# One order out of 401 planned ones, and a shorter way to split V, in a three-layer attention kernel

## The chip, the cores and the metric

One NeuronCore of one Trainium2 chip. The metric is the device time of one launch in microseconds (us). The kernel before took 1083.33 us (median of 3 runs, 1083.30 to 1086.17).

## The reference

Three layers follow each other, for 4 batches (b = 0..3) of 448 positions and a width of 768:

```python
scores = scale * np.matmul(q, k.transpose(0, 1, 3, 2))      # causal, 12 heads of 64
attn = softmax(mask(scores));  x = concat(attn @ v)          # 1. attention
h = xt @ U @ V;  u = x + h.T                                 # 2. low-rank mixing over positions
x = u + np.maximum(u @ w_ch1, 0.0) @ w_ch2                   #    and an MLP of 768 -> 3072 -> 768
logits = x @ w_gate;  top 2 of 4 experts                     # 3. each expert: one causal attention head
out += gate[e] * (softmax(mask(q @ k.T)) @ v) @ wo[e]
```

All is float32. The kernel multiplies in pieces of float16: a float32 operand is split into a high part (rounded to float16) and a low part (what is left), and three products of such parts (high*high, high*low, low*high) replace one.

## The kernel before

**Steps.** `ORDER` lists the work: `a0` to `a3` are the attention of a batch (`attention(b)`, six pairs of heads each, so pairs 0 to 23 in all), `mgb..` is weight group g (of 4) of the MLP for batches b (`mlp`), `s2` and `s3` are groups 2 and 3 for batches 2 and 3 together by a seven-product scheme (`strassen`), `e0` to `e3` are the experts. The list starts a0 a1 m00 m01 m101.

**A pair of heads** (`attention`, L693): the scores come from TensorE; VectorE adds the mask and takes the maximum (the profile's CUSTOM_DVE_ANT_0); ScalarE takes the exponential and copies the high part in float16; GpSimd subtracts for the low part (`softmax`, L512); two transposing DMAs from SP's queue turn the result. `prep(n)` (L490) splits V of the pair: ScalarE scales V in place (112x512), ScalarE copies the high part (112x8x64), GpSimd subtracts for the low part (112x8x64). `weighted` (L589) first calls `shares` (the reciprocals of the sums: small 112x8 operations on VectorE, 16 small matmuls of shape 64x112 on TensorE, one copy on ScalarE), then makes 24 products of V and the turned scores (64x448 to 64x112); VectorE multiplies the two, ScalarE and GpSimd split the result, and a transposing DMA and `lowrank(n)` (L606; 12 matmuls of 64x128, two ScalarE copies, 32x128 on VectorE, one more matmul) end the pair.

**Weights.** Each of the 48 weight tiles (`weight_tile`, L743) is loaded, decoded on VectorE (four passes of 128x768), squared on ScalarE, normed by a matmul of 128x1, scaled and rounded on ScalarE, and cut on GpSimd (two of 128x384). Tiles 0 to 11 (group 0) are due during the attention of batches 0 and 1.

**What sets the order.** No operation is issued when the code calls it. `Program.add` records it with its engine, its dependencies and a key (the due time, `prog.key`; `HT` = 4500 per half pair; matmuls of the MLP get `FILL`, a key so late that they go wherever nothing else is ready). `Program.issue` (L203) then runs a list schedule: it keeps a clock for each engine, made of `cost` (L125) and `LATENCY` (L59), always takes the engine that can start first, lets it issue its ready operation of the smallest key, and so lays down one fixed sequence per engine. On the chip every engine works through its sequence in order and waits on semaphores. Where the planned TensorE would idle for over 100 ns before 210 us (`WARM_END`, L43) the planner puts dummy matmuls of 128x448 into TensorE's sequence (L1248, called fillers below); they keep its clock up. The plan itself orders nothing across engines.

Of the kernel before, what the change touches and what calls it, by code (L numbers as in the profile page):

```python
# [3 lines left out]

# [42 lines left out]
NE = 6  # L47
ORDER = "a0 a1 m00 m01 m101 m20 m30 e0 a2 m21 m31 e1 a3 m02 m12 s2 s3 e2 m03 m13 e3"
NT = 2 * NG * GF + NE
PASS = [(0, 0), (0, 1), (1, 0)]  # L50


class Program:
# [2 lines left out]

    LATENCY = {"pe": 197.0, "act": 135.0, "dve": 185.0, "pool": 85.0, "sp": 1010.0}  # L59

    def __init__(self):
        self.ops = []
# [59 lines left out]
            self.state[r] = ([], [])  # L122
        return self.near[r]

    def cost(self, name, method, outs, ins, kw):  # L125
        o = outs[0]
        n = 1
        for c in o.shape[1:]:
            n *= c
        if name == "pe":  # L130
            f = 4.0 if ins[0].dtype == F32 else 1.0
            c = f * max(n / 2.4 + 2.5, 36.0)
            self.work = c * (ins[0].shape[0] / 128.0) * (o.shape[0] / 128.0)

            return c * (0.62 if HD in (o.shape[0], ins[0].shape[0]) and n >= C else 1.0)
        ptr = sum(x.free_size() == 1 and n > 1 for x in ins)
        psum = any(a.space == bass.MemoryType.PSUM for a in outs + ins)
        if name == "act" and method == "dma_start":
            return 300.0
        if name == "act":  # L140
            src = 51.0 if ins[0].space == bass.MemoryType.PSUM else 94.0
            return src + n / 1.2 + 93.0 * (ptr + len(outs) - 1)
        if name == "dve":
            m = 1
            for c in ins[0].shape[1:] if ins else o.shape[1:]:
                m *= c
# [3 lines left out]
            return (64.0 + (m / 2 if fast else m)) / 0.96 + 64.0 * ptr + 80.0 * (self.port and n > 32)  # L150
        if name == "pool":
            if method == "partition_all_reduce":
                return 374.0
            self.port = True
            return 150.0 + 2.0 * n if method == "tensor_tensor" else 260.0 + 2.5 * n
        return 350.0 + outs[0].nbytes() / 292.0 if method == "dma_start_transpose" else 650.0

    def add(self, name, method, fn, a, k):
        outs, ins = [], []
        for key, x in list(enumerate(a)) + list(k.items()):  # L160
            if hasattr(x, "ap"):
                (outs if key in (0, "out", "accum_out") else ins).append(x)
        self.work, self.port = 0.0, False
        cost = self.cost(name, method, outs, ins, k)
        data = 0.0
        if method.startswith("dma"):
            nbytes = max(x.nbytes() for x in outs + ins)
            data = nbytes / (292.0 if method == "dma_start_transpose" else 360.0)
        deps = set()
        i = len(self.ops)  # L170
        if self.group_op:
            i -= 1
        for x in ins:
            r = self.region(x)
            if r is not None:
                for q in self.touching(r):
                    deps.update(self.state[q][0])
                self.state[r][1].append(i)
        for x in outs:
            r = self.region(x)  # L180
            if r is not None:
                for q in self.touching(r):
                    w, rd = self.state[q]
                    deps.update(w)
                    deps.update(rd)
                    if q[1] >= r[1] and q[2] <= r[2] and q[3] >= r[3] and q[4] <= r[4]:
                        w[:] = [i]
                        rd[:] = []
        deps.discard(i)
        if self.group_op:  # L190
            op = self.ops[-1]
            op["calls"].append((fn, a, k))
            op["cost"] += cost
            op["work"] += self.work
            op["deps"] |= deps
        else:
            op = dict(eng=name, cost=cost, data=data, deps=deps, calls=[(fn, a, k)], key=self.key,
                      work=self.work, port=self.port)
            self.ops.append(op)
            if self.group_op is False:  # L200
                self.group_op = True

    def issue(self):  # L203
        ops = self.ops
        left = [len(o["deps"]) for o in ops]
        users = [[] for _ in ops]
        for i, o in enumerate(ops):
            for d in o["deps"]:
                users[d].append(i)
        at = [0.0] * len(ops)  # L210
        names = ["pe", "act", "dve", "pool", "sp"]
        free = dict.fromkeys(names, 0.0)
        bus = port = 0.0
        warm, window, load = False, 0.0, 0.0
        waiting = {n: [] for n in names}
        ready = {n: [] for n in names}
        for i, o in enumerate(ops):
            if not left[i]:
                heapq.heappush(waiting[o["eng"]], (0.0, i))
        done = 0  # L220
        while done < len(ops):
            best = None
            for n in names:
                t = free[n]
                while waiting[n] and waiting[n][0][0] <= t:
                    i = heapq.heappop(waiting[n])[1]
                    heapq.heappush(ready[n], (ops[i]["key"], i))
                if not ready[n]:
                    if not waiting[n]:
                        continue  # L230
                    t = waiting[n][0][0]
                if best is None or t < best[0]:
                    best = (t, n)
            t, n = best
            while waiting[n] and waiting[n][0][0] <= t:
                i = heapq.heappop(waiting[n])[1]
                heapq.heappush(ready[n], (ops[i]["key"], i))
            i = heapq.heappop(ready[n])[1]
            o = ops[i]
            if n == "pe" and self.idle and t < WARM_END:  # L240
                u = free[n] or WARM_START
                while u + WARM_GAP < t:
                    while u > window + WINDOW:
                        warm = load > (0.42 if warm else 0.76) * WINDOW
                        window, load = window + WINDOW, 0.0
                    self.idle()
                    c = 190.0 if warm else 380.0
                    u += c
                    load += c
                t = max(t, u)  # L250
            for fn, a, k in o["calls"]:
                fn(*a, **k)  # L252
            done += 1
            cost = o["cost"]
            if n == "pe":
                while t > window + WINDOW:
                    warm = load > (0.42 if warm else 0.76) * WINDOW
                    window, load = window + WINDOW, 0.0
                load += o["work"] * (1.0 if warm else 2.0)
                if not warm:  # L260
                    cost *= 2.0

            if o["port"]:
                t = max(t, port)
                port = t + cost
            end = t + cost
            free[n] = end
            if o["data"]:
                end = bus = max(bus, t + 1290.0) + o["data"]
                if n == "sp" and cost > 700.0:  # L270
                    free[n] = max(free[n], end - 1000.0)
            for u in users[i]:
                gap = 20.0 if n == "pe" and ops[u]["eng"] == "pe" else self.LATENCY["sp" if o["data"] else n]
                at[u] = max(at[u], end + gap)
                left[u] -= 1
                if not left[u]:
                    heapq.heappush(waiting[ops[u]["eng"]], (at[u], u))
        return max(free.values())


@with_exitstack
def kernel(
# [207 lines left out]
    def prep(n):  # L490
# [804 lines left out]
```

## Time and profile before

| | |
|---|---|
| Median of the runs | 1083.33 us |
| The profiled execution: time, span | 1087.6 us, 1085.6 us |
| Busy: TensorE / VectorE / ScalarE / GpSimd | 1043.5 / 695.1 / 639.6 / 484.7 us |
| of TensorE's busy time: fillers (L1248) | 436 matmuls, 96.2 us |
| Mean granted clock of TensorE | 0.995 |

The span runs from the first to the last instruction; the execution's time is 2 us longer. A busy TensorE is not a useful one here, since fillers count as busy. So the profile is read by stretches: up to 219.5 us (attention of batches 0 and 1 with group 0 for batch 0 between it), where fillers stand, and after it, where TensorE's own work follows without a break but for short waits.

### The profile page before, as it was taken

Reading aid. Unit: us, or ns where it says so; the run is one execution under the profiler, and the core shown is the slowest. Engines: PE = TensorE matmul, PEld = TensorE weight load, DVE = VectorE, ACT = ScalarE, POOL = GpSimd, SP = SyncE. Lnnn points to the kernel's source line nnn. Section 1 sums busy time; section 2 is a strip of 40 time slices with the busy share of each in tenths; the row PEclk is TensorE's granted clock in tenths of the full one; section 3 lists DMA queues with packets and bytes.
Section 4 is the critical chain, followed back from the end, with each engine's and each line's share of the span. In section 5 each row is a group of like instructions: output and inputs, shape, how many; then the busy total and the mean of one; then the engine's idle time right before and its main releaser. Section 6 shows DMA issues by size and latency. Waiting matters only on the chain.

```text
span 1085.6 us, 18934 instructions
## 1 busy us (share of the span) xinstructions
PE 1043.5 (96%) x6824; PEld 556.0 (51%) x6824; DVE 695.1 (64%) x1811; ACT 639.6 (59%) x1517; POOL 484.7 (45%) x528
## 2 busy tenths in 40 slices
PE   8999999999999999999999999999999999999996
PEld 3455454555545555554455554455455544555554
DVE  6778698878767677535566545577665768432363
ACT  3898998566754654447885448884462631631163
POOL 1777766325424331024563016674697992220011
PEclk9999999999999999999999999999999999999998
DMA  5999899746868876547997257995434444543024
GB/s 165 231 246 231 214 216 235 208 167 225 283 229 285 279 271 235 172 116 177 244 243 156 88 116 179 224 193 128 129 112 139 131 123 154 145 116 102 18 77 94
DMA packets 220141, 192.56 MB, mean 177 GB/s; under 512 B 176304, under 2 KB 179504, under 8 KB 220048
## 3 DMA queue, kind: packets, MB, share of 16 engines
q1 hardware_dynamic: 220048, 191.36, 64.7%
q8 instruction: 53, 0.87, 0.3%
q14 instruction: 40, 0.33, 0.1%
HBM read 112.16 MB, written 36.18 MB: 137 GB/s over the span
## 4 chain that ended last, share of the span: by engine, by line
PE 66%; DMA 14%; ACT 8%; POOL 5%; DVE 4%; issue 2%; SPq 0%; DVEq 0%; ACTq 0%; POOLq 0%
PE bank L252 62%; DMA arena<-arena 9%; ACT arena L252 8%; POOL arena L252 5%; PE bank L1248 4%; DVE arena L252 4%; DMA arena<-w 2%; DMA w<-arena 2%; DMA arena<-in_w_dram 1%; DMA arena<-in_wv_dram 1%; DMA arena<-in_v_dram 1%; DMA out_dram<-arena 0%; SPq L252 0%; DMA arena<-in_qk_dram 0%; ACT bank L252 0%
## 5 line engine op out<-in xcount | busy, mean ns | idle before, releaser
L252 PE MATMUL bank<-arena 128*128 128x448 f16 (+10 forms) x6388 | 957.7, 326 | 36.4 <-DMA arena<-arena 12.3
L252 POOL TENSOR_TENSOR arena<-arena 112x112 f16<-112x112 f32 (+8 forms) x517 | 482.5, 956 | 590.7 <-ACT arena L252 544.5
L252 PEld LDWEIGHTS <-arena 128*128 128x128 f16 (+4 forms) x5852 | 474.8, 104 | 430.0 <-issue 82.9
L252 ACT ACTIVATE arena<-arena 128x448 f16<-128x448 f32 (+11 forms) x895 | 492.8, 587 | 272.0 <-DVE arena L252 192.2
L252 DVE CUSTOM_DVE_ANT_0 arena<-bank,arena 112x112 f32<-112x112 f32 (+4 forms) x280 | 124.4, 476 | 71.9 <-PE bank L252 57.2
L252 DVE TENSOR_TENSOR arena<-bank,arena 128x448 f16<-128x448 f32 (+2 forms) x160 | 94.8, 600 | 117.3 <-ACT arena L252 90.9
L252 DVE SCALAR_TENSOR_TENSOR arena<-arena 128x768 int32<-128x768 int32 (+6 forms) x168 | 163.1, 988 | 2.0 <-ACT arena L252 0.9
L252 DVE SCALAR_TENSOR_TENSOR arena<-bank,arena 128x448 f32<-128x448 f32 (+1 forms) x138 | 84.2, 621 | 88.0 <-PE bank L252 69.2
L252 DVE TENSOR_SCALAR arena<-arena 128x1 int32<-128x1 int32 (+8 forms) x377 | 88.5, 258 | 41.2 <-ACT arena L252 15.6
L252 ACT ACTIVATE arena<-bank 128x448 f16<-128x448 f32 (+2 forms) x148 | 75.1, 520 | 59.7 <-PE bank L252 58.7
L252 DVE TENSOR_TENSOR arena<-arena 112x8 f16<-112x8 f32 (+10 forms) x136 | 88.5, 664 | 18.3 <-ACT arena L252 16.7
L1248 PE MATMUL bank<-arena 128*128 128x448 f16 x436 | 96.2, 362 | 1.9 <-DVE arena L1172 1.0
L252 ACT ACTIVATE arena<-bank,arena 64x128 f16<-64x128 f32 (+2 forms) x97 | 41.6, 433 | 56.3 <-PE bank L252 51.1
L252 ACT ACTIVATE bank<-bank,arena 128x448 f32<-128x448 f32 x72 | 43.0, 602 | 53.5 <-PE bank L252 52.2
L252 PEld LDWEIGHTS bank<-arena 64*112 64x112 f32 (+5 forms) x536 | 48.2, 173 | 48.3 <-issue 15.4
L1248 PEld LDWEIGHTS <-arena 128*128 128x128 f16 x436 | 40.9, 102 | 47.1 <-issue 14.8
L252 DVE TENSOR_REDUCE arena<-arena 128x1 f32<-128x448 f32 (+8 forms) x107 | 57.5, 545 | 6.8 <-DMA arena<-in_v_dram 2.9
L252 ACT ACTIVATION_READ_ACCUMULATOR arena<-arena 112x1 f32 (+1 forms) x304 | 57.4, 189 | 0.0
L252 DVE DVE_READ_ACCUMULATOR2_ANT arena<- 112x1 f32 (+1 forms) x280 | 22.9, 82 | 0.0
L252 DVE CAST arena<-arena 112x8 f16<-112x8 f32 x32 | 15.3, 483 | 2.2 <-PE bank L252 1.9
L252 DVE TENSOR_SCALAR arena<-bank 128x1 f32<-128x1 f32 x48 | 7.3, 152 | 12.7 <-PE bank L252 10.7
L252 DVE TENSOR_REDUCE arena<-bank 1x1 f32<-1x128 f32 (+2 forms) x14 | 3.9, 277 | 9.3 <-PE bank L252 9.2
(12 smaller groups left out, 17.7 us busy)
## 6 DMA issues: line engine op xcount, KB each, us to landing
arena<-w SPq DMA_DIRECT2D x138, 384.0 KB, 3.5
arena<-in_w_dram SPq DMA_DIRECT2D x48, 768.0 KB, 5.3
w<-arena SPq DMA_DIRECT2D x78, 384.0 KB, 4.3
arena<-in_qk_dram SPq DMA_DIRECT2D x24, 448.0 KB, 4.0
arena<-in_v_dram SPq DMA_DIRECT2D x24, 224.0 KB, 4.3
out_dram<-arena SPq DMA_DIRECT2D x24, 224.0 KB, 2.0
arena<-in_we_dram SPq DMA_DIRECT2D x6, 384.0 KB, 4.5
arena<-arena SPq DMA_TRANSPOSE x88, 4.7
```

Source lines behind the costliest of these rows:

```text
L252: fn(*a, **k)
L1248: prog.idle = lambda: nc.tensor.matmul(bank[:, 7, 64:512], ZERO.to_broadcast([128, 128]), ZERO.to_broadcast([128, S]), start=True, stop=True)
```

## The change

It has two parts.

1. `prep`: the in-place scaling of V on ScalarE and the subtraction on GpSimd go. `split` (L470 of before) does both steps from the loaded tile: ScalarE writes the high part with the scale, VectorE computes scale*V - high in one SCALAR_TENSOR_TENSOR of 112x8x64. Per pair: one ScalarE operation and one GpSimd operation less, one VectorE operation more; 24 pairs.
2. `Program`: `cost` and the latencies get other numbers, transposing DMAs get a model of their own, and each duration is taken times 1.03. The schedule moves into `plan(keys, users)`, which issues nothing and returns the planned end and the order. `issue` plans once, then 400 times more with the keys of 1 to 16 random groups of operations moved by random amounts (only keys of 0 to 270000, those of the attention, the weight tiles and the first steps of `strassen`), keeps the order with the earliest planned end, and issues that one. The random numbers have a fixed seed.

```diff
+STEP, MOVABLE, SEED, ROUNDS = 4500.0, 270000.0, 8, 400
...
-    LATENCY = {"pe": 197.0, "act": 135.0, "dve": 185.0, "pool": 85.0, "sp": 1010.0}
+    HOP = 66.0
+    SLACK = 1.03
...
-    def issue(self):
+    def plan(self, keys, users):
+
         ops = self.ops
...
+            cost, fill = o["cost"] * self.SLACK, 0
+            tail = o["tail"]
             if n == "pe":
+                if t < WARM_END:
+                    u = free[n]
+                    while u + WARM_GAP < t:
...
+                        fill += 1
+                        c = 190.0 if warm else 380.0
+                        u += c
+                        load += c
+                    t = max(t, u)
...
+    def issue(self):
+
+        ops = self.ops
...
+        best, order = self.plan(keys, users)
+        dice = random.Random(SEED)
+        for _ in range(ROUNDS):
+            trial = keys[:]
+            for _ in range(dice.choice((1, 2, 4, 16))):
+                by = dice.gauss(0.0, dice.choice((0.1, 0.5, 2.0))) * STEP
+                for i in dice.choice(parts):
+                    trial[i] = max(0.0, trial[i] + by)
+            end, made = self.plan(trial, users)
+            if end <= best:
+                best, order, keys = end, made, trial
+        for i, fill in order:
+            for _ in range(fill):
+                self.idle()
+            for fn, a, k in ops[i]["calls"]:
+                fn(*a, **k)
...
-        act.activation(vs, vs, AF.Copy, scale=SV[0:C, b:b + 1])
-        act.activation(dst[:, :, 0:64], src, AF.Copy)
-        pool.tensor_tensor(out=dst[:, :, 64:128], in0=src, in1=dst[:, :, 0:64], op=ALU.subtract)
+        split(dst[:, :, 0:64], dst[:, :, 64:128], src, SV[0:C, b:b + 1])
```

The program built from it has 401 fillers in place of 436, and the same 6120 other matmuls. Up to the 975th of these (the last one before group 0's work on batch 1) the sets are the same in both; their sequence is not. At three places:

ScalarE, the first two pairs, from the last small exponential on (112x224, 112x448: exponentials; 112x2x..x56: high parts; 112x512 and 112x8x64: V; 128x768: weight tile). Before:

```order
L252 ACTIVATE arena<-arena 112x224 x2
L252 ACTIVATE arena<-arena 112x2x2x56 x2
L252 ACTIVATE arena<-arena 112x512
L252 ACTIVATE arena<-arena 112x2x3x56
L252 ACTIVATE arena<-arena 112x8x64
L252 ACTIVATE arena<-arena 112x512
L252 ACTIVATE arena<-arena 112x2x3x56
L252 ACTIVATE arena<-arena 112x448 x2
L252 ACTIVATE arena<-arena 112x2x4x56
L252 ACTIVATE arena<-arena 128x768
L252 ACTIVATE arena<-arena 112x2x4x56
L252 ACTIVATE arena<-arena 112x8x64
```

and now:

```order
L324 ACTIVATE arena<-arena 112x8x64 x2
L324 ACTIVATE arena<-arena 112x224 x2
L324 ACTIVATE arena<-arena 112x2x2x56 x2
L324 ACTIVATE arena<-arena 128x768
L324 ACTIVATE arena<-arena 112x448
L324 ACTIVATE arena<-arena 112x2x3x56
L324 ACTIVATE arena<-arena 112x448
L324 ACTIVATE arena<-arena 112x2x3x56
L324 ACTIVATE arena<-arena 112x2x4x56
```

The scaling of V is gone, and V's high parts moved ahead of the larger exponentials.

VectorE, end of batch 1's attention, around pair 10's `lowrank` (32x128: its operand; the TENSOR_TENSOR just ahead of the ISA: the product of pair 11; the one ahead of that: a low part of the MLP; ISA 128x448: the sum of pair 10). Before:

```order
L252 SCALAR_TENSOR_TENSOR arena<-bank,arena 32x128
L252 COPY arena<-bank 128x1
L252 TENSOR_SCALAR arena<-bank 128x1
L252 SCALAR_TENSOR_TENSOR arena<-arena 128x768
L252 TENSOR_TENSOR arena<-bank,arena 128x448
L252 TENSOR_SCALAR arena<-arena 128x1 x2
L252 TENSOR_TENSOR arena<-bank,arena 128x448
L252 ISA arena<-bank,arena 128x448
```

and now:

```order
L324 SCALAR_TENSOR_TENSOR arena<-arena 128x768
L324 TENSOR_TENSOR arena<-bank,arena 128x448
L324 SCALAR_TENSOR_TENSOR arena<-arena 112x8x64
L324 SCALAR_TENSOR_TENSOR arena<-bank,arena 32x128
L324 TENSOR_TENSOR arena<-bank,arena 128x448
L324 ISA arena<-bank,arena 128x448
L324 ISA arena 128x1
L324 SCALAR_TENSOR_TENSOR arena<-arena 112x8x64
```

Two of the new subtractions (V of pairs of batch 2) stand here, one of them ahead of pair 10's 32x128.

TensorE, the same place (64x448 to 64x112 in one run: pair 11's products; 64x128: pair 10's `lowrank`; the later run of 64x112: pair 11's `shares`; 128x1: norm of a weight tile; 128x448: MLP). Before:

```order
L252 MATMUL bank<-arena 64x448
...
L252 MATMUL bank<-arena 64x128
L252 MATMUL bank<-arena 128x1
L252 LDWEIGHTS arena
L252 MATMUL bank<-arena 128x448
...
L252 MATMUL bank<-arena 128x1
...
L252 MATMUL bank<-arena 64x112
```

and now (L1292 are fillers):

```order
L324 MATMUL bank<-arena 64x112
L1292 LDWEIGHTS arena
L1292 MATMUL bank<-arena 128x448
...
L324 MATMUL bank<-arena 128x448
...
L324 MATMUL bank<-arena 64x128
...
L324 MATMUL bank<-arena 64x448
```

Pair 11's `shares` stood behind its products, behind pair 10's `lowrank` and behind two norms; it now stands ahead of all of them.

## Rows read from the trace of the kernel before

**Rows 1.** The page: span, then busy time, share and instructions of each engine.
```profile
span 1085.6 us, 18934 instructions
PE 1043.5 (96%) x6824; PEld 556.0 (51%) x6824; DVE 695.1 (64%) x1811; ACT 639.6 (59%) x1517; POOL 484.7 (45%) x528
```
**Rows 2.** The page's costliest groups: count, busy us, mean ns, idle before, releaser.
```profile
L1248 PE MATMUL bank<-arena 128*128 128x448 f16 x436 | 96.2, 362 | 1.9 <-DVE arena L1172 1.0
```
**Rows 3.** Busy time by stretch: length, each engine's busy us (instructions), clock, DMA share, GB/s.
```profile
20.00:182.30 162.30, 156.30 (x1215) 82.00 (x1214) 131.77 (x422) 145.52 (x405) 114.05 (x134) 1.00 0.94 218
0.00:219.50 219.50, 208.81 (x1535) 109.21 (x1536) 174.01 (x538) 173.61 (x453) 133.90 (x161) 1.00 0.90 219
219.50:1085.60 866.10, 834.68 (x5291) 446.82 (x5288) 521.08 (x1274) 466.00 (x1065) 350.81 (x367) 0.99 0.59 167
300.00:330.00 30.00, 28.27 (x146) 14.53 (x145) 21.18 (x53) 17.04 (x25) 11.31 (x11) 0.94 0.69 233
```
**Rows 4.** The chain of waits, 20 to 220 us: shares of the stretch.
```profile
by line: PE bank L252 34.0%; PE bank L1248 15.8%; DMA arena<-arena 14.1%; ACT arena L252 13.9%; POOL arena L252 10.5%; DVE arena L252 5.0%; issue 3.3%; DMA arena<-in_v_dram 2.8%; SPq L252 0.6%; ACTq L252 0.0%; POOLq L252 0.0%
```
**Rows 5.** ScalarE's and GpSimd's groups by shape, 20 to 210 us: V's three operations.
```profile
L252 ACT ACTIVATE arena<-arena 112x512 f32<-112x512 f32 x18 | 12.5, 709 | 0.3 <-DVE arena L252 0.3
L252 ACT ACTIVATE arena<-arena 112x512 f16<-112x512 f32 x14 | 8.5, 616 | 2.0 <-PE bank L252 2.0
L252 POOL TENSOR_TENSOR arena<-arena 112x512 f16<-112x512 f32 x14 | 17.2, 1233 | 1.1 <-ACT arena L252 1.1
```
**Rows 6.** VectorE's groups by shape, 20 to 210 us.
```profile
L252 DVE SCALAR_TENSOR_TENSOR arena<-arena 128x448 f16<-128x448 f32 x6 | 5.4, 904 | 0.6 <-ACT arena L252 0.5
L252 DVE CAST arena<-arena 112x8 f16<-112x8 f32 x12 | 8.8, 732 | 0.0
```
**Rows 7.** VectorE in order of time: start, length, instruction; the nearest kin of the new subtraction.
```profile
115.88 1.55 DVE L252 SCALAR_TENSOR_TENSOR arena<-arena 128x448 f16<-128x448 f32 x1
218.04 3.65 DVE L252 SCALAR_TENSOR_TENSOR arena<-arena 128x448 f16<-128x448 f32 x6
719.62 2.71 DVE L252 SCALAR_TENSOR_TENSOR arena<-arena 128x448 f16<-128x448 f32 x1
```
**Rows 8.** GpSimd in order of time, beside the first and third of rows 7.
```profile
114.81 3.24 POOL L252 TENSOR_TENSOR arena<-arena 128x448 f16<-128x448 f32 x4 [0.97 <-ACT arena L252]
718.97 4.25 POOL L252 TENSOR_TENSOR arena<-arena 112x336 f16<-112x336 f32 x4 [0.83 <-ACT arena L252]
```
**Rows 9.** TensorE by shape, 192.9 to 194.6 us: pair 11's products.
```profile
L252 PE MATMUL bank<-arena 112*64 112x448 f16 x6 | 1.2, 356 | 0.0
L252 PE MATMUL bank<-arena 112*64 112x112 f16 x6 | 0.7, 213 | 0.0
```
**Rows 10.** TensorE by shape, 196.85 to 197.6 us: pair 11's `shares`.
```profile
L252 PE MATMUL bank<-arena 112*64 112x112 f16 x16 | 0.6, 216 | 0.0
```
**Rows 11.** VectorE in order of time: the product of pair 11.
```profile
198.33 0.61 DVE L252 TENSOR_TENSOR arena<-bank,arena 128x448 f32<-128x448 f32 x1
```
**Rows 12.** TensorE in order of time, around the end of the first stretch.
```profile
215.31 1.12 PE L1248 MATMUL bank<-arena 128*128 128x448 f16 x5
216.36 0.38 PE L252 MATMUL bank<-arena 1*128 1x1 f32 x2
216.67 2.86 PE L1248 MATMUL bank<-arena 128*128 128x448 f16 x14
219.37 2.81 PE L252 MATMUL bank<-arena 128*128 128x448 f16 x14
```
**Rows 13.** TensorE's waits after 219.5 us: us in total, times, longest.
```profile
PE bank L252 <- ACT arena L252: 9.4, 11, 1.7
PE bank L252 <- DVE arena L252: 8.6, 6, 2.0
PE bank L252 <- DMA arena<-arena: 8.3, 9, 2.2
PE bank L252 <- DMA arena<-w: 1.2, 2, 0.8
```

More of the change, by code (lines that the diff above doesn't have):

```diff
@@ L216, in issue @@
         ready = {n: [] for n in names}
+        order = []
         for i, o in enumerate(ops):
@@ L219, in issue @@
                 heapq.heappush(waiting[o["eng"]], (0.0, i))
-        done = 0
-        while done < len(ops):
+        while len(order) < len(ops):
             best = None
@@ L224, in issue @@
                 t = free[n]
[L225 to L229, printed above, removed]
+                w, r = waiting[n], ready[n]
+                while w and w[0][0] <= t:
+                    i = heapq.heappop(w)[1]
+                    heapq.heappush(r, (keys[i], i))
+                if not r:
+                    if not w:
                         continue
-                    t = waiting[n][0][0]
+                    t = w[0][0]
                 if best is None or t < best[0]:
@@ L234, in issue @@
             t, n = best
[L235 to L238, printed above, removed]
-            o = ops[i]
[L240 to L254, printed above, removed]
-            if n == "pe":
+            w, r = waiting[n], ready[n]
+            while w and w[0][0] <= t:
+                i = heapq.heappop(w)[1]
+                heapq.heappush(r, (keys[i], i))
+            i = heapq.heappop(r)[1]
+            o = ops[i]
+            cost, fill = o["cost"] * self.SLACK, 0
+            tail = o["tail"]
+            if n == "pe":
+                if t < WARM_END:
+                    u = free[n]
+                    while u + WARM_GAP < t:
+                        while u > window + WINDOW:
+                            warm = load > (0.42 if warm else 0.76) * WINDOW
+                            window, load = window + WINDOW, 0.0
+                        fill += 1
[3 more added lines that the diff above has]
+                    t = max(t, u)
                 while t > window + WINDOW:
@@ L265, in issue @@
                 port = t + cost
[L266 to L271, printed above, removed]
+            free[n] = t + cost
+            end = t + cost + tail
+            if o["turns"]:
+                behind = turn > t
+                free[n] = max(t + 120.0, plain + 60.0, turn - 700.0 if behind else 0.0)
+                end = max(free[n] + 250.0, turn) + o["data"]
+                if behind:
+                    free[n] = max(free[n], end - 1800.0)
+                turn = end
+                bus = max(bus, end + 400.0)
+            elif o["data"]:
+                bus = max(bus, t + 1050.0) + o["data"]
+                end = bus + 850.0
+                plain = max(plain, end)
@@ L278, in issue @@
-        return max(free.values())
+                    heapq.heappush(waiting[e], (at[u], u))
+        return last, order
+    def issue(self):
+        ops = self.ops
+        users = [[] for _ in ops]
+        parts = {}
+        for i, o in enumerate(ops):
+            for d in o["deps"]:
+                users[d].append(i)
+            if 0.0 <= o["key"] < MOVABLE:
+                parts.setdefault((o["eng"], o["key"]), []).append(i)
+        parts = list(parts.values())
+        keys = [o["key"] for o in ops]
+        best, order = self.plan(keys, users)
[14 more added lines that the diff above has]
+                fn(*a, **k)
```

68 lines of the change are left out of this document (37 added, 31 removed).

## The prediction

> **What bounds the kernel now.** I read the page first, for the span and the busy times [rows 1]. TensorE is 96% busy, but 96.2 us of that are fillers [rows 2]. So I next took the busy times by stretch [rows 3], cut where the fillers end. Up to 219.5 us TensorE is busy for 208.8 us; without the fillers its own work is 112.6 us, and 10.7 us are idle in spite of them. That stretch costs 219.5 us for 112.6 us of work: it is bound by something else. After it, 834.7 of 866.1 us are work. The 31.4 us that are left are small waits [rows 13], the longest of 2.2 us. Whatever the change wins must therefore come from the 107 us in the first stretch that are not work, or from these 31 us.
>
> What sets the length of the first stretch? The chain of waits there [rows 4] holds, beside TensorE and its fillers, transposing DMAs (14%), ScalarE (14%), GpSimd (10.5%) and VectorE (5%): it runs through the pairs of heads, each handing its tiles around all engines, with two or three pairs under way. From 20 to 182.3 us, where the last pair's high parts are copied, ScalarE is busy 145.5 of 162.3 us, 90%; VectorE 131.8 (81%); GpSimd 114.1 (70%) [rows 3]. ScalarE sets the pace, and at 90% hardly more is to be had out of an engine whose work arrives in pieces. The end of the stretch is the end of batch 1's attention plus what follows from it (`split_u`, then group 0 on batch 1): 14 fillers run just ahead of that work [rows 12], so TensorE had nothing else left.
>
> **Part 1, the split of V.** Twelve pairs lie in the first stretch. ScalarE loses the scaling in place, 0.709 us, and its copy of the high part, 0.616 us, now carries the scale; I take the 0.709 us of the scaled form of the same shape for it [rows 5]. That is 0.616 us less for each pair, 7.4 us in all. GpSimd loses 1.233 us for each pair [rows 5], 14.8 us in all, or 13% of its 114.1 us.
>
> VectorE gains twelve subtractions of 112x8x64. The trace of before has no such one. The nearest row is the same instruction with the same types at 128x448 [rows 6]: 0.904 us, times 512/448 is 1.03 us (an estimate, as are the next ones). Alone it takes 0.61 us (six in 3.65 us), so 0.70 us is the low end. One of 1.55 us and one of 2.71 us [rows 7] lie inside unbroken runs of GpSimd [rows 8]; scaled they are 1.77 and 3.1 us. I take 1.03 us, since it is the mean over this very stretch: 12.4 us in all, between 8.4 and 21.2 us if I let the 1.55 us be the usual case. GpSimd's lighter load gives a little back: a CAST of eight columns takes VectorE 0.732 us here [rows 6], most of which must be waiting. I count 1 us for that.
>
> Rows 7 and 8 show VectorE's instruction stretched when GpSimd works. The Trainium skill, "SBUF — State Buffer", section "Who interferes with whom", says why: a VectorE instruction with two SBUF inputs contends with a GpSimd instruction that reads SBUF, and the second one to issue is blocked until the first finishes. It speaks against moving this subtraction to VectorE while GpSimd still does the other low parts; it also says that the operation taken away, on GpSimd, held VectorE up. What follows if each one is blocked is the slower rival below.
>
> Now the pace. If ScalarE still sets it at the 90% of today, 138.1 us of work take 154.0 us instead of 162.3: 8.3 us less. If VectorE sets it at that share, 131.8 + 12.4 - 1.0 = 143.2 us take 159.6 us: 2.7 us less. These are the two ends for part 1.
>
> The other twelve pairs (batches 2 and 3) run while TensorE has MLP work in its sequence, so the same savings there cost and bring nothing; the cover is the MLP, 834.7 of 866.1 us. Were it gone, the same 2.7 to 8.3 us would be won there once more.
>
> **Part 2, the order.** Two things can be read off. First, where a step moved. Before, pair 11's products were done by 194.6 us [rows 9], but `shares` came on TensorE only at 196.9 us [rows 10], behind pair 10's `lowrank` and two norms, so that VectorE multiplied at 198.33 us [rows 11]. That is 3.7 us on the chain that ends the stretch. Now `shares` stands ahead. Against it, pair 10's `lowrank` (twelve small matmuls, under 1 us) and one of the new subtractions (1.03 us on VectorE) have moved ahead of that product. I count 2 us won.
>
> Second, the fillers. They are instructions, and each one will be run. At 96.2/436 = 0.22 us [rows 2], 35 fewer are 7.7 us. Since the first stretch is work + fillers + idle, and the work up to its end is the same 975 matmuls, it becomes 112.6 + 88.5 + idle. With the 10.7 us idle of today it ends at 211.8 us. It ends later by whatever the plan left out.
>
> The two ways agree: 2.7 to 8.3 us from part 1 and 2 us from the order make 4.7 to 10.3 us, in the middle 7.5; the fillers say 7.7. I take 7.5 us.
>
> What it meets next: group 0 on batch 1 follows at once, its weights long in place, and the groups after it have their tiles as late or as early as before, since these too are made after the stretch. For the 31.4 us of waits after 219.5 us [rows 13] the new plan deals new cards: TensorE works in order, and one tiny matmul that waits for ScalarE or VectorE holds up all behind it. I see no reason for a sum in either direction and take zero, with a third of it, 10 us, as the bound on both sides. One fall of the clock is in there (0.94 over 30 us [rows 3], 1.8 us of work lost); it may go or come back elsewhere.
>
> The profiled execution took 1087.6 us, 4.3 us above the median of the runs, and its span is 1085.6. The gain is a difference within it, so I take it off the median: 1083.3 - 7.5 = 1075.8 us.
>
> **Rivals.**
>
> *VectorE becomes the bound (slower).* It stands at 81%, and the new subtraction stands in its in-order sequence ahead of mask, `shares` and `lowrank`, for all of which TensorE or ScalarE wait. If every one is stretched like the 1.55 us row, to 1.77 us, VectorE has 131.8 + 21.2 = 153.0 us, at 90% in 170.6 us: 8.3 us longer, 1091.6 us. It decides from (162.3 x 0.897 - 131.8)/12 = 1.15 us for each. For it: GpSimd is still busy 60% of the time. Against it: that share falls, and the mean in this stretch is 0.9 us, not 1.55. By the rule of the Trainium skill's page named above, taken to the full, each one would be blocked for a GpSimd instruction, and it is this case. Chance 0.11.
>
> *The order does not hold on the chip (about the same).* The 35 fillers go, but idle takes their place, because the plan's durations are wrong in the places that matter, or the time won is lost to new waits after 219.5 us. For it: even now 10.7 us of idle stand beside 436 fillers, and 31.4 us later on were not planned. Against it: the ScalarE and GpSimd work is gone whatever the plan thinks. It leaves 0 to 3 us of gain, 1080.5 to 1083.5 us. Chance 0.15.
>
> *The later waits shrink too (faster still).* A plan with better durations places the tiny matmuls where their inputs are ready. A third of 31.4 us less, on top of 7.5: 1083.3 - 7.5 - 10 = 1066 us. For it: these waits are of just the kind that a plan can avoid. Against it: most keys that the search may move belong to the attention and the weight tiles, and TensorE's last 45 us keep nearly their sequence. Chance 0.14.
>
> **How the numbers follow.** The forecast, 4 to 11 us faster (1072 to 1079), has 0.60. A measurement of this kernel can tell about 0.3%, 3.2 us, from no change. Faster by more: the forecast and the third rival, and a little of the second: 0.76. Within: most of the second, 0.13. Slower: 0.11. The range goes from 1066 (half of the third rival left out) to 1084 us (the second one held, the slower one left out).
>
> **What would show it.** In the profile after: fillers 401, some 88 us; the first stretch's end (the last fillers, then group 0 on batch 1 without a break) near 212 us; ScalarE still the busiest of the three from 20 us to the last high parts, VectorE near it; the new subtraction at about 1.0 us there; idle beside the fillers about 11 us; some 31 us of idle after. The step on part 1 is wrong if VectorE is over 90% busy and its subtractions take over 1.2 us; the step on the order, if the idle beside the fillers grows by several us; the zero for the rest, if the idle after the stretch is not within 25 to 37 us.

## The result

The changed kernel takes 1074.0 us against 1083.3 us (medians of six runs each); the means stand in a ratio of 0.9899, with a 95% interval of 0.987 to 0.9928. The forecast was 1075.8 us. The time came out close to it, but the sum behind it did not: the first stretch gave twice what was forecast, and part of that is not to be found in the medians.

The page of the kernel after, its first two parts and the fillers' group of its fifth, to be held against [rows 1, 2]:

```profile
span 1065.0 us, 18851 instructions
PE 1034.2 (97%) x6789; PEld 551.1 (52%) x6789; DVE 711.6 (67%) x1835; ACT 630.2 (59%) x1493; POOL 464.6 (44%) x504
L1292 PE MATMUL bank<-arena 128*128 128x448 f16 x401 | 88.2, 360 | 2.0 <-DVE arena L324 1.0
```

The 401 fillers take 88.2 us, as forecast. The span is 20.6 us shorter than that of before, more than the 9.3 us of the medians: the profiled execution of before (1087.6 us) lies 4.3 us above its median, that of after (1066.7 us) 7.3 us below. An identical kernel, run again, had 1071.4 us and a span of 1071.7 us.

Busy time by stretch of the kernel after, as [rows 3] (length, busy us of PE, PEld, DVE, ACT and POOL with their instructions, clock, DMA share, GB/s). The first row ends with the copy of the last pair's high parts, at 182.9 us before and 171.0 us now ([rows 3] stop at 182.3 us, where the last of these copies begins; ScalarE's share before is 90% either way); the other two are cut where group 0 on batch 1 begins:

```profile
20.00:171.00 151.00, 148.41 (x1186) 77.21 (x1184) 134.87 (x419) 138.08 (x390) 104.45 (x123) 1.00 1.01 233
0.00:205.30 205.30, 201.02 (x1500) 103.98 (x1501) 177.23 (x550) 162.99 (x434) 121.20 (x147) 1.00 0.96 232
205.30:1065.00 859.70, 833.16 (x5291) 447.15 (x5289) 534.37 (x1286) 467.23 (x1060) 343.44 (x357) 1.00 0.59 169
```

The first stretch ends at 205.3 us, 14.1 us earlier. TensorE is busy there for 201.0 us, of which 88.2 are fillers, so its own work is 112.8 us, as before. The fillers lost 8.0 us, the idle time fell from 10.7 to 4.3 us, and that is the 14.1 us (with rounding). ScalarE is busy for 138.1 of 151.0 us (91%), VectorE for 134.9 (89%).

TensorE in order of time at the end of the stretch (start, length, instruction), as [rows 12]:

```profile
190.56 14.29 PE L324 MATMUL bank<-arena 128*64 128x128 f16 x84 [0.58 <-DMA arena<-arena]
204.68 0.74 PE L1292 MATMUL bank<-arena 128*128 128x448 f16 x3
205.26 19.98 PE L324 MATMUL bank<-arena 128*128 128x448 f16 x110
```

Before, 14 and 5 fillers stood here; now three, and ahead of them 14 us of work without a break. The chain of waits from 20 to 205 us shows who is late now, as [rows 4]:

```profile
by line: PE bank L324 48.2%; PE bank L1292 26.0%; DVE arena L324 16.3%; DMA arena<-arena 6.3%; POOL arena L324 1.4%; ACT arena L324 1.3%; issue 0.5%; DVEq L324 0.0%
```

ScalarE and GpSimd, 14% and 10.5% before, have all but left the chain; VectorE has gone from 5 to 16%. The waits of TensorE after the stretch (us in total, times, longest), as [rows 13]:

```profile
PE bank L324 <- DMA arena<-arena: 11.3, 10, 2.0
PE bank L324 <- DVE arena L324: 6.2, 6, 2.0
PE bank L324 <- ACT arena L324: 4.2, 7, 1.6
PE bank L324 <- POOL arena L324: 0.8, 1, 0.8
```

They are 22.7 us up to the last matmul, against 27.6 us before; 3.8 us more lie behind the last matmul in both. And V's operations by shape, 20 to 196 us, as [rows 5] (count, busy us, mean ns):

```profile
L324 DVE SCALAR_TENSOR_TENSOR arena<-arena 112x512 f16<-112x512 f32 x14 | 11.5, 820 | 0.6 <-ACT arena L324 0.6
L324 ACT ACTIVATE arena<-arena 112x512 f16<-112x512 f32 x14 | 9.9, 713 | 2.3 <-DVE arena L324 1.7 <-PE bank L324 0.5
```

The subtraction takes 0.82 us, less than the 1.03 us forecast; the copy with the scale in it takes the 0.71 us assumed.

### The profile page after: what moved, and what is told of

Read it like the earlier page. It is cut to its first block, busy times and chain, and to the rows that moved or that the text cites. A ratio compares the mean times of both kernels' runs of the same rounds, so it can differ in the third digit from the quotient of the medians.

```text
span 1065.0 us, 18851 instructions
## 1 busy us (share of the span) xinstructions
PE 1034.2 (97%) x6789; PEld 551.1 (52%) x6789; DVE 711.6 (67%) x1835; ACT 630.2 (59%) x1493; POOL 464.6 (44%) x504
## 4 chain that ended last, share of the span: by engine, by line
PE 74%; DMA 10%; DVE 6%; ACT 5%; POOL 3%; issue 2%; SPq 0%; POOLq 0%; DVEq 0%; ACTq 0%
PE bank L324 69%; DMA arena<-arena 6%; PE bank L1292 6%; DVE arena L324 6%; ACT arena L324 5%; POOL arena L324 3%; DMA arena<-in_w_dram 2%; DMA w<-arena 1%; DMA arena<-w 0%; DMA arena<-in_qk_dram 0%; ACT bank L324 0%; SPq L324 0%; POOLq L1334 0%; DVEq L324 0%; POOLq L324 0%
## 5 line engine op out<-in xcount | busy, mean ns | idle before, releaser
L324 PE MATMUL bank<-arena 128*128 128x448 f16 (+11 forms) x6388 | 956.2, 325 | 25.0 <-DMA arena<-arena 11.9
L324 POOL TENSOR_TENSOR arena<-arena 128x384 f16<-128x384 f32 (+8 forms) x493 | 462.4, 958 | 590.2 <-ACT arena L324 532.9
L324 PEld LDWEIGHTS <-arena 128*128 128x128 f16 (+5 forms) x5852 | 473.5, 104 | 422.1 <-issue 74.1
L324 ACT ACTIVATE arena<-arena 128x768 f16<-128x768 f32 (+14 forms) x871 | 481.6, 587 | 231.4 <-DVE arena L324 144.8
L324 DVE SCALAR_TENSOR_TENSOR arena<-arena 128x768 int32<-128x768 int32 (+7 forms) x192 | 180.0, 954 | 4.3 <-ACT arena L324 3.2
L324 DVE CUSTOM_DVE_ANT_0 arena<-bank,arena 112x224 f32<-112x224 f32 (+4 forms) x280 | 125.8, 475 | 64.5 <-PE bank L324 47.7
L324 DVE TENSOR_SCALAR arena<-arena 128x1 int32<-128x1 int32 (+9 forms) x377 | 87.6, 257 | 43.3 <-ACT arena L324 16.2
L324 DVE TENSOR_TENSOR arena<-arena 112x8 f16<-112x8 f32 (+10 forms) x136 | 90.3, 682 | 12.8 <-ACT arena L324 10.8
L1292 PE MATMUL bank<-arena 128*128 128x448 f16 x401 | 88.2, 360 | 2.0 <-DVE arena L324 1.0
L1292 PEld LDWEIGHTS <-arena 128*128 128x128 f16 x401 | 37.0, 101 | 43.4 <-issue 13.6
L324 DVE DVE_READ_ACCUMULATOR2_ANT arena<- 112x1 f32 (+1 forms) x280 | 22.7, 81 | 0.0
L324 DVE RECIPROCAL arena<-arena 112x8 f32<-112x8 f32 (+1 forms) x36 | 7.0, 195 | 0.5
```

The source lines that it names most:

```text
L1292: prog.idle = lambda: nc.tensor.matmul(bank[:, 7, 64:512], ZERO.to_broadcast([128, 128]), ZERO.to_broadcast([128, S]), start=True, stop=True)
```

## The experiments

For every kernel the table gives, from its profiled execution, the fillers, the end of the first stretch (the start of TensorE's 976th matmul that is not a filler), the idle time in it, and for the rest up to the last matmul its length, split into TensorE's busy and idle time; then the span, and the median and ratio to before from the timed runs. The ratio, with its 95% interval, is formed from all timed runs and not from the medians. The end of a stretch comes from one execution, but after and again, which are the same kernel, agree on it within 0.3 us; the rest and the medians move by several us from run to run.

| kernel | fillers | stretch ends | idle in it | rest = busy + idle | span | median | ratio |
|---|---|---|---|---|---|---|---|
| before | 436 | 219.4 | 10.7 | 862.4 = 834.8 + 27.6 | 1085.6 | 1083.3 | |
| after | 401 | 205.3 | 4.3 | 855.9 = 833.2 + 22.7 | 1065.0 | 1074.0 | 0.9899 [0.987, 0.9928] |
| again | 401 | 205.5 | 4.4 | 862.4 = 838.1 + 24.3 | 1071.7 | 1071.4 | 0.9891 [0.986, 0.9922] |
| split_only | 431 | 220.3 | 12.6 | 860.4 = 837.0 + 23.4 | 1084.5 | 1084.2 | 1.0004 [0.9978, 1.0029] |
| plan_only | 433 | 212.6 | 6.9 | 865.4 = 838.7 + 26.7 | 1081.8 | 1090.0 | 1.0062 [1.0034, 1.009] |
| no_search | 428 | 216.5 | 10.0 | 867.3 = 838.6 + 28.7 | 1087.5 | 1092.0 | 1.0093 [1.0057, 1.0128] |
| new_v_same_order | 436 | 217.5 | 9.8 | 858.3 = 833.4 + 24.9 | 1079.5 | 1085.4 | 1.0022 [0.9999, 1.0044] |
| old_v_same_order | 401 | 208.4 | 6.4 | 860.5 = 835.9 + 24.6 | 1073.1 | 1074.9 | 0.9926 [0.9904, 0.9949] |
| v_twice | 401 | 212.2 | 7.6 | 861.9 = 837.6 + 24.3 | 1077.9 | 1079.8 | 0.9973 [0.9955, 0.999] |
| half_fill | 184 | 205.5 | 31.6 | 862.4 = 838.9 + 23.5 | 1071.7 | 1072.6 | 0.991 [0.9882, 0.9937] |
| seed1 | 428 | 219.0 | 10.1 | 863.3 = 839.2 + 24.1 | 1086.0 | 1088.0 | 1.0048 [1.0028, 1.0069] |
| seed10 | 392 | 211.9 | 10.8 | 870.2 = 841.2 + 29.0 | 1085.8 | 1084.2 | 0.9999 [0.9969, 1.0029] |
| seed14 | 390 | 203.4 | 5.2 | 876.3 = 845.3 + 31.0 | 1083.5 | 1079.9 | 0.9966 [0.9946, 0.9985] |
| seed23 | 395 | 205.8 | 6.3 | 869.8 = 842.0 + 27.8 | 1079.5 | 1080.1 | 0.9956 [0.993, 0.9982] |

**Each part alone, each planned by its own planner.** Part 1 in the kernel before:

```diff
-        act.activation(vs, vs, AF.Copy, scale=SV[0:C, b:b + 1])
-        act.activation(dst[:, :, 0:64], src, AF.Copy)
-        pool.tensor_tensor(out=dst[:, :, 64:128], in0=src, in1=dst[:, :, 0:64], op=ALU.subtract)
+        split(dst[:, :, 0:64], dst[:, :, 64:128], src, SV[0:C, b:b + 1])
```

> The kernel before with part 1 of the change alone (V split by ScalarE and VectorE), planned by the old planner; 431 fillers. Theory A (the work taken off ScalarE and GpSimd sets the pace of the pairs, part 1 carries most of the gain): 5 to 8 us faster than before, first stretch near 213 us. Theory B (the durations and the search carry the gain): within 3 us of before, fillers as many as before.

Part 2 alone is the kernel after with the same edit the other way round:

> The changed kernel with V split the old way (ScalarE scales and copies, GpSimd subtracts), planned by the new planner with its search; 433 fillers. Theory A: 2 to 4 us faster than before. Theory B: 6 to 9 us faster. If the two parts only work together, both this and split_only are within 3 us of before.

And the kernel after with its first schedule, without the 400 trials:

```diff
-STEP, MOVABLE, SEED, ROUNDS = 4500.0, 270000.0, 8, 400
+STEP, MOVABLE, SEED, ROUNDS = 4500.0, 270000.0, 8, 0
```

> The changed kernel with the first of the 401 plans (ROUNDS = 0): new durations, V split the new way, no search; 428 fillers in place of 401. If the search is worth what its fillers say (27 fewer, 0.22 us each), the first stretch is 6 us longer than in the changed kernel, 211 us, and the time 1080 us; if the search only fits the plan's own errors, the time is that of the changed kernel, 1074 us.

None of the three is faster than before. split_only came as theory B had it; plan_only is 6.7 us slower, where 2 to 9 us faster or no difference over 3 us were named, and no_search lies above both of its values. Busy time from 20 us to the last high parts, of split_only and of no_search:

```profile
20.00:184.70 164.70, 156.65 (x1229) 82.30 (x1228) 134.17 (x427) 137.51 (x387) 104.67 (x123) 1.00 0.96 213
```

```profile
20.00:181.50 161.50, 154.34 (x1215) 81.10 (x1215) 142.89 (x428) 139.41 (x391) 104.70 (x123) 1.00 0.94 219
```

In split_only ScalarE has 8.6 us less to do than before (137.5 for 146.1), and the high parts end 1.8 us later: its share simply falls from 90 to 83%. The old planner made another order for it, so this run alone does not separate the two; in the unchanged order, below, the same exchange ends the stretch 1.9 us earlier. ScalarE did not set the pace: an engine is not the bound because it is 90% busy. In no_search VectorE is at 88% and ScalarE at 86%, and the stretch ends at 216.5 us. The search among orders, with the seed of the kernel after, takes that to 205.3 us. With what it does to the rest it is worth 18 to 21 us of the median (1092.0 to 1074.0 or 1071.4), more than the whole gain. plan_only ends its stretch 6.8 us earlier than before and is still 0.6% slower. Its profiled execution, 1083.6 us, is the fastest of its runs, so its trace does not show where its median loses; that stays open. Beside old_v_same_order below, which carries out the same operations in another order, it shows something else: the order that was planned for the other split of V ends the stretch 4.2 us earlier (208.4 for 212.6 us) and has a median 15 us shorter (1074.9 for 1090.0 us) than the one planned for these very operations. So the plan does not tell which order is the faster on the chip.

**Part 1 in a fixed order.** Here the order of all instructions stays as another kernel planned it, and only what V's three operations call is exchanged. The new split in the order of before:

```diff
+        scale_op, hi_op, lo_op = prog.ops[-3:]
+        s = SV[0:C, b:b + 1]
+        scale_op["calls"] = []
+        hi_op["calls"] = [(nc.scalar.activation, (dst[:, :, 0:64], src, AF.Copy), dict(scale=s))]
+        lo_op["calls"] = [(nc.vector.scalar_tensor_tensor, (), dict(out=dst[:, :, 64:128], in0=src, scalar=s,
+                                                                    in1=dst[:, :, 0:64], op0=ALU.mult, op1=ALU.subtract))]
```

> The sequence of the kernel before on every engine, fillers too, with V split the new way in the same places: ScalarE's scaling is left out, its copy carries the scale, VectorE subtracts where GpSimd did. The reverse exchange in the changed order cost 3.0 us of the first stretch (208.4 against 205.4 us). If the work taken off ScalarE and GpSimd is worth as much in either order: first stretch 216.4 us, time 1080 us. If the old order waits elsewhere and cannot use it: 219 to 220.5 us, time 1083 us, as with split_only.

The old split in the order of after:

```diff
+        hi_op, lo_op = prog.ops[-2:]
+        hi_op["calls"] = [(nc.scalar.activation, (vs, vs, AF.Copy), dict(scale=SV[0:C, b:b + 1])),
+                          (nc.scalar.activation, (dst[:, :, 0:64], src, AF.Copy), {})]
+        lo_op["calls"] = [(nc.gpsimd.tensor_tensor, (), dict(out=dst[:, :, 64:128], in0=src, in1=dst[:, :, 0:64],
+                                                             op=ALU.subtract))]
```

> The changed kernel's sequence on every engine, with V split the old way in the same places: ScalarE scales V in place and copies the high part where it now only copies, GpSimd subtracts where VectorE did. If ScalarE's time sets the pace of the pairs, the 0.6 us for each of twelve pairs come back: first stretch 210 to 213 us. If the order alone carries the gain and leaves enough slack on ScalarE and GpSimd, 205 to 207 us.

In the order of before the new split ends the stretch 1.9 us earlier (no gain in the medians), in the order of after 3.1 us earlier (208.4 to 205.3; the medians differ by 1 to 3.5 us and the intervals overlap). Both ends lie between the values that were named. So part 1 by itself is worth 2 to 3 us of the first stretch, and the order, with the old split in it, 11.0 us of its 14.1 (of the median 8.5 us). In old_v_same_order the last product of 112x448 of the sixth pair ends 6.7 us earlier than before (106.5 for 113.2 us), that of the ninth 8.6 us, that of the last 10.7 us (183.6 for 194.3 us); at the fourth pair there is no gain. Which moves in the order bring this is not shown.

VectorE's price is the surprise. Busy time of the whole first stretch, of new_v_same_order and then of before; VectorE (the third pair of numbers) runs the same instructions in the same order, and 14 subtractions more, the twelve of the first stretch's pairs and two that belong to the next ones:

```profile
0.00:217.50 217.50, 207.66 (x1535) 108.29 (x1536) 175.23 (x552) 164.94 (x435) 120.34 (x147) 1.00 0.90 221
```

```profile
0.00:219.40 219.40, 208.71 (x1535) 109.15 (x1536) 173.91 (x538) 173.51 (x453) 133.90 (x161) 1.00 0.90 219
```

VectorE's busy time rises by 1.3 us, although the subtractions alone take 11.9 us. The rest comes back from its other instructions. By shape, 20 to 208 us of new_v_same_order, then 20 to 210 us of before:

```profile
L252 DVE SCALAR_TENSOR_TENSOR arena<-arena 128x768 int32<-128x768 int32 x30 | 31.9, 1066 | 0.1
L252 DVE SCALAR_TENSOR_TENSOR arena<-arena 112x512 f16<-112x512 f32 x14 | 11.9, 849 | 0.0
L252 DVE TENSOR_SCALAR arena<-arena 128x768 int32<-128x768 int32 x15 | 9.6, 645 | 0.0
L252 DVE CAST arena<-arena 112x8 f16<-112x8 f32 x12 | 7.3, 611 | 0.0
L252 DVE TENSOR_TENSOR arena<-arena 112x8 f16<-112x8 f32 x12 | 5.0, 416 | 0.0
```

```profile
L252 DVE SCALAR_TENSOR_TENSOR arena<-arena 128x768 int32<-128x768 int32 x30 | 35.4, 1184 | 0.1
L252 DVE TENSOR_SCALAR arena<-arena 128x768 int32<-128x768 int32 x15 | 10.9, 731 | 0.0
L252 DVE TENSOR_TENSOR arena<-arena 112x8 f16<-112x8 f32 x12 | 7.4, 617 | 0.0
```

With the CAST of [rows 6] (8.8 us before) these four groups give back 3.5, 1.3, 1.5 and 2.4 us, 8.7 us in all, with not one instruction less. In the order of after it is much the same: from old_v_same_order, whose first stretch follows, to after VectorE's busy time rises by 3.1 us (174.1 to 177.2) for 14 subtractions of 11.5 us.

```profile
0.00:208.40 208.40, 201.99 (x1499) 103.91 (x1500) 174.12 (x536) 170.03 (x448) 135.04 (x161) 1.00 0.92 229
```

What changed beside these groups from before to new_v_same_order is GpSimd, 13.6 us less busy (133.9 to 120.3), and ScalarE, 8.6 us less (173.5 to 164.9). The traces point to GpSimd. Two CASTs of before, the first just ahead of the GpSimd row at 114.81 us in [rows 8], the second inside the unbroken GpSimd work of the last row:

```profile
114.64 0.17 DVE L252 CAST arena<-arena 112x8 f16<-112x8 f32 x1
154.76 2.38 DVE L252 CAST arena<-arena 112x8 f16<-112x8 f32 x1
152.57 5.90 POOL L252 TENSOR_TENSOR arena<-arena 112x448 f16<-112x448 f32 x7 [1.32 <-ACT arena L252]
```

Of the 30 SCALAR_TENSOR_TENSOR of 128x768, those that no GpSimd instruction overlaps take 0.94 to 0.96 us (6 of them before, 9 in new_v_same_order), those that lie wholly inside GpSimd's work 1.38 us on average before and 1.24 us in new_v_same_order (10 and 9). The TENSOR_TENSOR of 112x8 takes 0.15 to 0.16 us where GpSimd is idle (none of the twelve before, four in new_v_same_order) and up to 1.08 us beside it. ScalarE does not sort them so: before, the passes of 128x768 average 1.17 us where it is busy for over 90% of their time, and 1.23 us where it is for at most half. The Trainium skill, "SBUF — State Buffer", section "Who interferes with whom", makes an overlap with GpSimd cost VectorE time where VectorE needs the port pair that the two share, as with two SBUF inputs, or with casts and tensor_scalar in a two-port mode. The rows agree in direction for all four shapes, by 10 to 33%; in which mode the CAST and the TENSOR_SCALAR ran, no row shows.

Then the subtraction doubled, in the order of after, to see whether VectorE is near its limit now:

```diff
+        prog.ops[-1]["calls"] *= 2
```

> The changed kernel with each of VectorE's new subtractions done twice in its place, all else and the order as it is: twelve more of 0.82 us in the first stretch, 9.8 us. VectorE is busy 133.1 of 148.7 us between 20 us and the last high parts there. If VectorE now sets the pace, the stretch gets 8 to 11 us longer, 213 to 216 us, and the slower rival was close; if it has slack at these places, 205.5 to 208 us.

```profile
20.00:177.70 157.70, 152.27 (x1192) 78.12 (x1191) 145.62 (x438) 138.53 (x391) 107.24 (x123) 0.99 0.94 223
```

VectorE's work up to the last high parts grows by 10.8 us (134.9 to 145.6), this stretch by 6.7 us, the end of the first stretch by 6.9 us, and the median by 6 to 8 us. The 212.2 us are just below what was named for VectorE setting the pace: some two thirds of its added time are on the path. The clock fell once in this stretch (0.66 from 115 to 120 us, 1.7 us of work lost), so that share may be a little smaller. In this order VectorE is close to the bound. But two subtractions take 1.7 us for each pair here (24 take 20.5 us), more than the 1.15 us from which the slower rival was to decide, and the kernel is still not slower than before (ratio 0.9973, stretch 212.2 for 219.4 us).

**The fillers.** The sum of part 2 took each of them as an instruction that costs its time.

```diff
-            for _ in range(fill):
+            for _ in range(fill // 2):
```

> The changed kernel's order with each row of fillers cut to half (184 fillers in place of 401). In the trace of the changed kernel 26% of the chain between 20 and 205 us is fillers. If they hold TensorE back, the first stretch gets shorter, 198 to 203 us. If TensorE would wait at the same places anyway, it ends at 204 to 206 us. If the clock falls without them, it gets longer than 206 us and the granted clock is below 0.95 in it.

And the kernel after unchanged, beside it:

> The changed kernel once more, for the spread of its runs (1066.7 to 1077.9 us so far, with the granted clock between 0.989 and 0.998) and for a second trace. If the spread is the clock, a slower run shows more stretches at the lower level, after 205 us, and the first stretch ends at 205 us as before; if it is the first stretch, that ends later.

half_fill's fillers on its page, then its busy time by stretch, and TensorE in order of time ahead of the second of these rows:

```profile
L1292 PE MATMUL bank<-arena 128*128 128x448 f16 x184 | 49.5, 391 | 2.3 <-DVE arena L324 1.3
```

```profile
0.00:205.50 205.50, 173.90 (x1282) 88.89 (x1283) 180.08 (x549) 161.67 (x433) 122.62 (x147) 0.97 0.94 231
37.00:44.00 7.00, 7.00 (x44) 3.69 (x39) 4.95 (x21) 5.01 (x12) 3.82 (x4) 0.51 1.05 278
```

```profile
32.89 0.35 PE L324 MATMUL bank<-arena 112*64 112x448 f16 x1 [1.16 <-DMA arena<-arena]
35.76 3.97 PE L324 MATMUL bank<-arena 112*64 112x448 f16 x33 [2.52 <-DMA arena<-arena]
```

With 184 fillers in place of 401 the stretch ends at the same 205.5 us: 27 us of idle, and 12 us by which TensorE's own work takes longer, have taken the place of 39 us of fillers. The clock falls to its lower level (0.51 from 37 to 44 us, that is 1.2 of 2.4 GHz, after two waits for DMAs of 1.2 and 2.5 us), here and at two more places of this stretch, and the end of the stretch does not move for that either: TensorE is ahead of what it waits for. The median is within 1.5 us of those of after and again. So these 217 fillers filled time that is waited for anyway. Their number is a reading of the idle time that the plan left; their time is not a cost.

**Other orders of the same kind.** Only the seed of the search differs (8 in the kernel after):

```diff
-STEP, MOVABLE, SEED, ROUNDS = 4500.0, 270000.0, 8, 400
+STEP, MOVABLE, SEED, ROUNDS = 4500.0, 270000.0, 14, 400
```

> The changed kernel with other random numbers in the search (SEED 1 in place of 8, 400 trials as before): 428 fillers, as many as without a search. Theory S (the search finds orders that are shorter on the chip, and the fillers that its plan still needs tell by how much): first stretch near that of the kernel without a search, 215 to 217 us, time 1082 to 1090 us. Theory P (any searched plan is as good, since what matters are the durations): 1074 us.

> The changed kernel with SEED 14: 390 fillers, 11 fewer than with SEED 8. Theory S: first stretch 202 to 204 us, time 1068 to 1073 us, a little faster than the changed kernel or the same. Theory L (SEED 8 was lucky on the chip, and fillers tell nothing): 1078 to 1090 us.

> The changed kernel with SEED 23, whose plan has 395 fillers and nearly the planned end of the changed one. What the search shortens is the first stretch: 203 to 207 us here. The part after it is dealt anew: between 856 and 876 us in the traces so far, so 1066 to 1083 us in all; near 1072 us if the 876 us of SEED 14 was the exception.

> The changed kernel with SEED 10: 392 fillers, the same planned end. First stretch 202 to 206 us, the rest 856 to 876 us, 1066 to 1082 us in all.

None of the four is as fast as seed 8. seed1 and seed10 end the first stretch later than was expected (219.0 us for 215 to 217, 211.9 us for 202 to 206), seed10 with nine fillers fewer than seed 8: the number of fillers does not tell where the stretch ends. seed14 came out as theory S had it in the stretch and as theory L had it in the time; seed23 lies within what was named for it. These two end the first stretch about as early as seed 8 (203.4 and 205.8 us), and yet their medians are 6 to 9 us longer. Their rest is 7 to 20 us longer. Of seed14's 20.4 us against after, 8.3 are idle time and 12.1 are TensorE's busy time for the same matmuls. Two stretches of seed14, and TensorE in order of time in them:

```profile
350.00:370.00 20.00, 16.68 (x83) 8.53 (x82) 14.07 (x33) 12.93 (x22) 8.45 (x8) 0.91 0.72 268
705.00:745.00 40.00, 34.03 (x276) 19.60 (x275) 29.04 (x58) 27.20 (x65) 21.65 (x22) 0.91 0.71 155
```

```profile
360.95 5.35 PE L324 MATMUL bank<-arena 128*128 128x1 f32 x20 [3.32 <-ACT arena L324]
712.08 7.13 PE L324 MATMUL bank<-arena 128*64 128x128 f16 x65 [2.59 <-DMA arena<-arena]
739.59 5.75 PE L324 MATMUL bank<-arena 128*64 128x128 f16 x42 [2.21 <-DMA arena<-arena]
```

One small matmul waits 2 to 3 us for ScalarE or a DMA and holds up all behind it, and at these places the mean clock is 0.91: three falls to 1.2 GHz begin right at the end of these stalls. Over the rest of this execution the lower level holds for 27.3 us in all, in after's for 3.4, in again's for 13.7. At half the speed 23.9 us more are 11.9 us lost, close to the 12.1 us of busy time. The same accounts for the two executions of the identical kernel: 10.2 us more at the lower level are 5.1 us lost, and the busy time differs by 4.9 us. So the rest varies by several us between executions of one order, and with the order on top of that; seed 8's is the best of the five orders run here.

## Why the prediction came out

**The split of the span** (own work, fillers, idle; what follows is TensorE-bound) held: own work was 112.8 us for 112.6 us, and what the order won lies in the first stretch.

**The pace of part 1** failed. "If ScalarE still sets it at the 90% of today" gave 8.3 us; VectorE's pace gave 2.7 us. The measured 1.9 to 3.1 us are at VectorE's end, but VectorE does not explain it in the order of before: its work grew by 1.3 us, where 11.4 us net had been counted up to the last high parts, and ScalarE's fell to 87% of its stretch with little won. In an order planned for the old durations the freed time probably lies where nothing stands ready to use it; this is not shown.

**The price of the subtraction** was 0.82 us for 1.03: in after the five of the fourteen that no GpSimd instruction overlaps take 0.74 us, and the three wholly inside GpSimd's work 0.95 us on average, so GpSimd's stretching was there, but small. More important is "I count 1 us" for what GpSimd's lighter load gives back: it is 8.7 us in the four groups alone.

**The fillers**: 401 and 88 us came as written, and 8.0 us less for them is near the 7.7. The argument was wrong all the same: each one is run, but that the stretch gets shorter by the time of those left out does not follow, since half_fill leaves out 217 and ends at the same place. The agreement of the two ways of reckoning was no confirmation.

**"With the 10.7 us idle of today"** is the mis-sized term. It was 4.3 us. With the fillers that makes 14.1 us for the 7.5 forecast. The order is worth 11.0 us of it (old_v_same_order against before) where 2 us were read off one moved step. That step did what was expected of it: VectorE multiplies for pair 11, as in [rows 11], 0.04 us after the products end (180.63 us), where 3.7 us lay between them before.

```profile
180.67 0.62 DVE L324 TENSOR_TENSOR arena<-bank,arena 128x448 f32<-128x448 f32 x1 [1.47 <-PE bank L324]
```

But from the end of these products to the end of the stretch it is 24.6 us now and was 24.8 us before: what was won there is lost again behind it, and the 14 us were won along the pairs ahead of it.

**Zero for the rest**, with 10 us on both sides, was right in size for this seed (855.9 and 862.4 us now, 862.4 before; idle to the end of the span 26.5 us, within the 25 to 37 named). The other seeds show that the bound was rather too narrow: up to 14 us more than before (seed14). Two readings behind it were off: 3.8 of the 31.4 us lie behind the last matmul and are no waits, and the trace of before holds a second fall of the clock (0.52 from 1069 to 1076.1 us). The third rival did not come about; the waits fell by 3 to 5 us. **The median** gives 9 to 12 us of the stretch's 14. The profiled execution of before was 4.3 us slower than its median, and its first stretch would hardly vary by that much, as the two traces of the same kernel after do not; so its rest is likely the part that was long. This is inferred, from one trace of before.

**The slower rival** had a mechanism that exists and a point of decision, 1.15 us, that the measured 0.82 us did not reach. v_twice shows that some two thirds of each further microsecond of VectorE would have been paid for, and that the rival's time, 1091.6 us, would not have come even at 1.7 us for each pair (1079.8 us): it left out what the order wins.

**The number was in part luck.** The forecast for the first stretch, 7.5 us, was half of the 14.1 us measured, and the median gives less than the stretch. And nothing in the forecast depends on the seed: with the four other seeds the time is 1079.9 to 1088.0 us, each beyond the forecast 1072 to 1079 us, and for two of them beyond 1084 us, the end of the whole range. What was right without luck is where the gain would come from, and that the work in the stretch stays the same.

No kernel run here beats the changed one by more than the runs scatter: half_fill and again are the same in time.

## What to carry to other kernels

A busy share of 90% does not make an engine the bound: take work off it in a fixed order, and again in the new order, before its time is counted as won. An order that a plan calls best is one draw: run several seeds, and judge each by the first stretch and by the rest, since a stall of 2 to 3 us at one small matmul there costs more than itself. When moving work from GpSimd to VectorE, look at VectorE's total, not at the price of the moved instruction.

## What was not expected of the hardware

Taking 14 subtractions (13.6 us) off GpSimd made VectorE's other instructions 8.7 us shorter in these four groups, 112x8 ones among them (617 to 416 ns); such a one takes 0.15 us where GpSimd is idle and up to 1.08 us beside it. And 39 us less of fillers' matmul time, with the clock at 0.97 in place of 1.00 over the stretch, did not move its end by more than 0.2 us.
